# Softplus in one ScalarE instruction, and attention visits moved to odd half steps

## The chip, the cores and the metric

The kernel runs on one core of one Trainium2 chip. TensorE (PE; its weight loads are listed as PEld), VectorE (DVE), ScalarE (ACT), GpSimd (POOL) and SyncE (SP, which here only issues DMAs) each run their own instruction stream in order; semaphores tie the streams together. The metric is the device time of one execution in microseconds (us), as the median of several runs. The profile shows one execution; its times are counted from the first instruction.

## The reference

Sliding-window attention feeds a two-layer network without any normalisation in between:

```
q, k, v: 8 batches x 8 heads x 576 positions x 64
scores = q @ k.T / 8;  heads 0-3: window of 32; heads 4-7: window of 128, every 4th key
attn   = softmax(masked scores);  x = attn @ v, rearranged to 4608 tokens x 512

h  = x @ w_in                                   # 4608 x 2048
sp = max(h, 0) + log1p(exp(-|h|))               # softplus(h)
g  = h * erf(sp)
out = g @ w_out                                 # 4608 x 512
```

## The kernel before

**The network.** Tokens are cut into 9 chunks of 512. The 2048 hidden features are cut into 8 pairs of 128-wide tiles (`PAIR = 2`). One step `t` computes one such pair of tiles for one chunk; there are 72 steps (`STEPS`): the first half of chunk 0's pairs, all of chunk 1, the second half of chunk 0, and then chunks 2 to 8, eight steps each. A step consists of two half steps `j = 0, 1`. The main loop counts half steps as `x = 2t + j`, so even `x` is the first half of a step and odd `x` the second. Weights and activations are split into a high and a low part in fp32r, and each product is made of three matmuls (high x high, high x low, low x high).

In half step `x` the program issues, in this order on each engine:

- the first matmul of step `t`: `mm1` (L517) for chunks 0 to 2, or `mm1_fast` (L638) from chunk 3 on, which combines seven block products (a Strassen-like scheme) and needs 24 matmuls in the even half step and 18 in the odd one. The first half step of `mm1_fast` is x = 48;
- `take` (L659) or `take_fast` (L647 to L652), by which VectorE brings `h` out of PSUM into the tile `hc`. `h` is one PSUM tile, so that the next half step's first matmul waits for it;
- in even half steps `exponents` (L246, ScalarE): the softmax exponentials of the attention units that were scored before;
- in odd half steps `table(t - 1)` (L667, ScalarE): the erf of the step before;
- `turn` (L264, L268): transposes of the probabilities of the units that are ready, and their copy;
- `normalize` (L257, L258 on VectorE, L259 on GpSimd) of units whose exponentials are done; a unit that will be transposed in the next half step (`due`) is normalised at the end of this one;
- `gate` (L674, L677, L678, VectorE): `h * erf(...)`, split into `ghi` and `glo`;
- in odd half steps `argument(t)` (L663, L664, ScalarE);
- `weights` (`prep_act`: a cast, L440, and an Abs, L445, on ScalarE; `prep_dve`: L454 to L460 on VectorE), the 32 pieces of weight preparation, one piece per half step, done by x = 31;
- the second matmul `mm2(t - 2, j)` (L692, 12 matmuls into the accumulators `acc`), and a `store` of the output at a chunk's end;
- `attend`: `values` (L283) of the units that are ready, `scores` (L225) of new units, and `rows_hi` (L325, ScalarE), which brings the attention rows out of PSUM;
- `load_left`, `right(x)` and `build(x)`: DMA loads and preparation of the operands of `mm1_fast`. `right` makes a chunk's right-hand operands at fixed places, by x modulo 16: loads at 8, VectorE differences (L604) at 10 and 11, ScalarE casts (L608) at 11 and 12, VectorE remainders (L613) at 12, 13 and 14;
- the DMA loads `load_qk`, `load_v` of later units, `mask_max` (L236, VectorE: mask and row maximum) of the units just scored, and `rows_lo` (L331, VectorE).

In the first two steps (x = 0 to 3) the order differs: `turn` and `weights` come before the first matmul, and `attend` comes before `argument`.

**The attention.** It is cut into 72 units. Visit `n` scores unit `n` and finishes unit `n - 3` (`LAG = 3`: transposes, values, rows). Visits 0 to 13 run ahead of the main loop (`first_visit`). The function `visits` places the others by hand into half steps of the main loop: single visits 14 to 23 into x = 0 to 6, 9, 11 and 14, and after that pairs of visits. A pair scores two units and finishes two. Visits 72 to 74 only finish units.

**The activation.** Before the change, softplus is made by ScalarE as -ln(sigmoid(-h)): a Sigmoid (L663) and a logarithm (L664) over a 128x1024 tile, and the erf (L667) takes the negated argument.

Of the kernel before, what the change touches and what calls it, by code (L numbers as in the profile page):

```python
# [14 lines left out]
AF = mybir.ActivationFunctionType  # L15
# [8 lines left out]
NBLK = S // BLK  # L24
# [17 lines left out]
NU = NIT * NBLK // PER  # L42
# [8 lines left out]
REBASE = 2.0 ** -112  # L51


TINY = 1.0e-12


PAIR = 2
SPC = FT // PAIR
HALF = SPC // 2
# [6 lines left out]
LAG = 3  # L66
# [17 lines left out]
BUILD = 2 * SPC * 2 - 1  # L84
READY = 8

ANCHORS = [(0, 31), (1, 33), (2, 35), (3, 37), (4, 39), (8, 55), (13, 71), (17, 87), (22, 103)]


def paced(k):  # L90
    for (a, x), (b, y) in zip(ANCHORS, ANCHORS[1:]):
        if k <= b:
            return x + (y - x) * (k - a) // (b - a)


def visits():


    at = {n - FIRST: [n] for n in range(FIRST, 2 * NBLK + LAG)}
    n, x = 2 * NBLK + LAG, 2 * HALF + 1  # L100
    for k in range(3):
        at[x + 5 * k // 2] = [n + k]
    for k in range(3):
        at[x + 9 + 5 * k] = [n + 3 + 2 * k, n + 4 + 2 * k]
    for k, n in enumerate(range(3 * NBLK + LAG, NU + LAG, 2)):
        x = paced(k)

        at[x - (x % (2 * SPC) == 0)] = [i for i in (n, n + 1) if i < NU + LAG]
    return at


# [37 lines left out]
def attn_moe_kernel(ctx: ExitStack, tc: tile.TileContext, qk, v, masks, eye, w_in, w_out, out):  # L149
    nc = tc.nc  # L150
# [320 lines left out]
    at = {0: [[x[:, i, 0:TOK] for x in xs] for i in range(2)]}  # L471
# [182 lines left out]
    hs, ls, gs = {}, {}, {}  # L654
# [5 lines left out]

    def argument(t):

        nc.scalar.activation(out=ls[t], in_=hs[t], func=AF.Sigmoid, scale=-1.0)  # L663
        nc.scalar.activation(out=ls[t], in_=ls[t], func=AF.Ln, bias=TINY)  # L664

    def table(t):
        nc.scalar.activation(out=ls[t], in_=ls[t], func=AF.Erf, scale=-1.0)  # L667

    def gate(t, j):

# [63 lines left out]
    with tc.manual_schedule():  # L734
# [11 lines left out]
        rows_lo(FIRST - 1 - LAG)  # L746

        plan = visits()


# [9 lines left out]
        for x in range(2 * (NT + 2)):  # L760
            t, j = divmod(x, 2)
            ns = plan.get(x, [])
# [29 lines left out]
            if j == 1 and 1 <= t <= NT:  # L792
                table(t - 1)
# [12 lines left out]
            if j == 1 and t < NT:  # L806
                argument(t)
# [113 lines left out]
```

## Time and profile before

| what | value |
|---|---|
| median of 3 runs | 916.88 us (915.61 to 917.37) |
| the profiled execution: its own time | 915.3 us |
| the profiled execution: span from first to last instruction | 913.5 us |
| granted TensorE clock, mean | 0.998 |
| busy: PE / PEld / DVE / ACT / POOL | 879.1 / 756.6 / 676.9 / 663.8 / 74.3 us |

A line of a group reads: line, engine, operation, output <- input, shape, count, then busy time in all and mean ns of one, then idle time of the engine just before them and what ended it. A line of a timeline reads: start, duration, engine, line, operation, count, and in brackets the idle time before it and what ended it. A line of a table of stretches reads: the stretch in us, its length, busy time (and number of instructions) of PE, PEld, DVE, ACT and POOL, the granted TensorE clock, the DMA share and GB/s. The profile's matmuls are pipelined and their ends are modelled; so lengths of half steps are taken below from start to start of their first matmuls.

### The profile page before, as it was taken

The page shows a single profiled execution, that of the slowest core. Times are in us where ns is not written, and L with a number is a line of the kernel's source. Part 1 is how long each engine was busy: PE and PEld are TensorE (multiplying, and loading weights), DVE is VectorE, ACT ScalarE, POOL GpSimd, SP SyncE. Part 2 cuts the span into 40 slices and gives each one's busy share as a digit, 9 for nine tenths or more (in the row PEclk, how much of TensorE's full clock was granted, in tenths as well). Part 3 has the DMA queues.
Part 4 walks back from the last instruction along what each step waited for, and adds up shares of the span by engine and source line. Part 5 has one row for each costly group of instructions (what it writes and reads, how often), then busy time and mean ns, then how long its engine had stood idle before and what let it go on. Part 6 is the DMA issues. An engine that isn't in the chain of part 4 may idle for free.

```text
span 913.5 us, 22874 instructions
## 1 busy us (share of the span) xinstructions
PE 879.1 (96%) x9072; PEld 756.6 (83%) x9072; DVE 676.9 (74%) x1773; ACT 663.8 (73%) x1324; POOL 74.3 (8%) x92
## 2 busy tenths in 40 slices
PE   4788999999999999999999999999999999999998
PEld 3566877888887878888889988888988999998996
DVE  6879989986788888767776777677666866776555
ACT  7779888885878797767976687769655756655553
POOL 2311100000011100000000000000100000000000
PEclk9999999999999999999999999999999999999999
DMA  8885544531759688676657765786566546655521
GB/s 298 282 275 184 182 163 138 158 121 53 250 187 330 217 301 305 249 270 236 215 197 280 263 208 202 278 289 225 171 233 226 189 140 237 231 178 206 198 82 46
DMA packets 74059, 194.00 MB, mean 212 GB/s; under 512 B 10464, under 2 KB 22496, under 8 KB 67808
## 3 DMA queue, kind: packets, MB, share of 16 engines
q1 hardware_dynamic: 73664, 192.02, 61.6%
q8 instruction: 71, 1.16, 0.5%
q10 hardware_dynamic: 288, 0.52, 0.1%
q14 instruction: 36, 0.29, 0.1%
HBM read 155.94 MB, written 35.65 MB: 210 GB/s over the span
## 4 chain that ended last, share of the span: by engine, by line
PE 79%; DVE 9%; ACT 7%; issue 2%; DMA 1%; POOL 1%; SPq 0%; DVEq 0%; ACTq 0%; POOLq 0%
PE acc L692 36%; PE h L638 14%; PE h L517 11%; PE tx L638 10%; PE sp L283 3%; PE sp L225 3%; ACT prob L246 1%; PE sp L264 1%; DVE prob L236 1%; DMA dbl<-in_w_in_dram 1%; DVE s L674 1%; ACT L667 1%; ACT s L664 1%; DVE w L459 1%; ACT s L663 1%
## 5 line engine op out<-in xcount | busy, mean ns | idle before, releaser
L692 PE MATMUL acc<-wout_hi,ghi 128*128 128x512 f32 x576 | 228.6, 397 | 0.4 <-DVE ghi L677 0.2
L692 PE MATMUL acc<-wout_lo,ghi 128*128 128x512 f32 x576 | 225.7, 392 | 0.0
L663 ACT ACTIVATE s<-hc 128x1024 f32<-128x1024 f32 x72 | 76.3, 1060 | 171.3 <-DVE hc L652 147.7
L692 PE MATMUL acc<-wout_hi,glo 128*128 128x512 f32 x576 | 159.0, 389 | 0.0
L692 PEld LDWEIGHTS acc<-wout_hi,glo 128*128 128x128 f32 x576 | 108.1, 188 | 22.8
L692 PEld LDWEIGHTS acc<-wout_hi,ghi 128*128 128x128 f32 x576 | 108.6, 189 | 20.7 <-DVE ghi L677 1.0
L692 PEld LDWEIGHTS acc<-wout_lo,ghi 128*128 128x128 f32 x576 | 108.6, 189 | 19.6
L259 POOL TENSOR_TENSOR prob<-prob,rinv 128x256 f32<-128x256 f32 x72 | 67.8, 950 | 536.2 <-DVE ssum L257 300.8
L678 DVE TENSOR_TENSOR glo<-s,ghi 128x512 fp32r<-128x512 f32 x144 | 100.0, 694 | 5.1
L674 DVE TENSOR_TENSOR s<-hc,s 128x1024 f32<-128x1024 f32 x72 | 92.3, 1282 | 14.1 <-ACT s L667 13.9
L517 PE MATMUL h<-x,win 128*128 128x512 f32 x384 | 99.5, 402 | 2.7 <-DVE hc L659 2.6
L246 ACT ACTIVATE prob<-prob,nmax 128x64 f32<-128x64 f32 x288 | 96.3, 337 | 2.9 <-DVE nmax L236 2.6
L638 PE MATMUL h<-win 128*128 128x256 f32 x720 | 98.1, 283 | 0.0
L667 ACT ACT_TABLE_LOAD x72 | 92.4, 1283 | 1.3
L664 ACT ACT_TABLE_LOAD x72 | 92.4, 1283 | 1.3
L638 PEld LDWEIGHTS h<-win 128*128 128x128 f32 x720 | 91.6, 192 | 0.0
L517 PEld LDWEIGHTS h<-x,win 128*128 128x128 f32 x384 | 73.2, 193 | 19.4 <-DVE hc L659 3.5
L667 ACT ACTIVATE s<-s 128x1024 f32<-128x1024 f32 x72 | 76.4, 1061 | 0.8
L664 ACT ACTIVATE s<-s 128x1024 f32<-128x1024 f32 x72 | 76.3, 1059 | 0.8
L236 DVE CUSTOM_DVE_ANT_0 prob<-sp,cst 128x64 f32<-128x64 f32 x288 | 45.6, 219 | 36.1 <-ACT rows L325 26.0
L677 DVE CAST ghi<-s 128x512 fp32r<-128x512 f32 x144 | 68.1, 473 | 2.5
L651 DVE TENSOR_TENSOR hc<-tx,hc 128x512 f32<-128x512 f32 x48 | 33.0, 688 | 40.4 <-PE tx L638 40.0
(102 smaller groups left out, 1270.3 us busy)
## 6 DMA issues: line engine op xcount, KB each, us to landing
win<-ws SPq DMA_DIRECT2D x48, 1024.0 KB, 5.6
win<-ws SPq DMA_DIRECT2D x48, 768.0 KB, 4.4
v<-in_v_dram SPq DMA_DIRECT2D x72, 256.0 KB, 4.3
qk<-in_qk_dram SPq DMA_DIRECT2D x48, 272.0 KB, 4.0
dbl<-in_w_in_dram SPq DMA_DIRECT2D x16, 512.0 KB, 4.6
dbl<-in_w_out_dram SPq DMA_DIRECT2D x16, 512.0 KB, 3.6
ws<-x SPq DMA_DIRECT2D x32, 256.0 KB, 4.7
qk<-in_qk_dram SPq DMA_DIRECT2D x24, 288.0 KB, 4.5
```

The lines of the kernel that those rows point to most:

```text
L236: nc.vector.tensor_tensor_reduce(out=pr[:, g, :], in0=sps[h][:, u % 2, p, :], in1=mask[QUADS.index(kinds(u, p))], scale=-SCALE, scalar=BIG ...
L246: nc.scalar.activation(out=probs[u][:, j, :], in_=probs[u][:, j, :], func=AF.Exp, scale=-1.0, bias=nmax[:, j:j + 1], accum_out=sums[u][:, ...
L259: nc.gpsimd.tensor_tensor(probs[u], probs[u], rinv.broadcast_to([P, 2 * PARTS, KEYS]), op=ALU.mult)
L517: nc.tensor.matmul(h, win_at[:, ftp, j, cc // 2, w, cc % 2, :], x[cc], start=(k == 0 and i == 0), stop=(k == CC - 1 and i == 2))
L638: nc.tensor.matmul((h, bank)[b][:, half * HN:(half + 1) * HN], w[:, k, wi, c, :], x[:, xi, c, :], start=(c == 0 and n == 0), stop=(c == 1 ...
L663: nc.scalar.activation(out=ls[t], in_=hs[t], func=AF.Sigmoid, scale=-1.0)
L664: nc.scalar.activation(out=ls[t], in_=ls[t], func=AF.Ln, bias=TINY)
L667: nc.scalar.activation(out=ls[t], in_=ls[t], func=AF.Erf, scale=-1.0)
L674: nc.vector.tensor_tensor(out=e, in0=hc, in1=e, op=ALU.mult)
L677: nc.vector.tensor_copy(out=ghi, in_=e[:, j])
L678: nc.vector.tensor_tensor(out=glo, in0=e[:, j], in1=ghi.bitcast(F32), op=ALU.subtract)
L692: nc.tensor.matmul(acc[tt], g[:, tt * P:(tt + 1) * P], w[:, ft, :], start=(first and w is wout_hi and g is ghi), stop=(last and g is glo))
```

## The change

`argument` becomes one ScalarE instruction with the function Softplus, on `hc` itself, and `table` takes its result without the sign. The plan of visits is written out as a list `PACE` of odd half steps. The pairs that stood in even half steps or were shifted by the rule at chunk ends move: the pair of visits 24, 25 from x = 18 to 19; 28, 29 from 28 to 27; 48, 49 from 58 to 59; 52, 53 from 63 to 65; 66, 67 from 90 to 91; 70, 71 from 95 to 97. All other visits keep their half step.

```diff
-TINY = 1.0e-12
...
-ANCHORS = [(0, 31), (1, 33), (2, 35), (3, 37), (4, 39), (8, 55), (13, 71), (17, 87), (22, 103)]
...
+PACE = [19, 23, 27, 31, 33, 35, 37, 39, 43, 47, 51, 55, 59, 61, 65, 67, 71, 75, 79, 83, 87, 91, 93, 97, 99, 103]
...
-    for k in range(3):
-        at[x + 9 + 5 * k] = [n + 3 + 2 * k, n + 4 + 2 * k]
-    for k, n in enumerate(range(3 * NBLK + LAG, NU + LAG, 2)):
-        x = paced(k)
-
-        at[x - (x % (2 * SPC) == 0)] = [i for i in (n, n + 1) if i < NU + LAG]
+    for x, n in zip(PACE, range(n + 3, NU + LAG, 2)):
+        at[x] = [i for i in (n, n + 1) if i < NU + LAG]
...
     def argument(t):
 
-        nc.scalar.activation(out=ls[t], in_=hs[t], func=AF.Sigmoid, scale=-1.0)
-        nc.scalar.activation(out=ls[t], in_=ls[t], func=AF.Ln, bias=TINY)
+        nc.scalar.activation(out=ls[t], in_=hs[t], func=AF.Softplus)
 
     def table(t):
-        nc.scalar.activation(out=ls[t], in_=ls[t], func=AF.Erf, scale=-1.0)
+        nc.scalar.activation(out=ls[t], in_=ls[t], func=AF.Erf)
```

More of the change, by code (lines that the diff above doesn't have):

```diff
@@ L85 @@
 READY = 8
-ANCHORS = [(0, 31), (1, 33), (2, 35), (3, 37), (4, 39), (8, 55), (13, 71), (17, 87), (22, 103)]
[L90 to L93, printed above, removed]
+PACE = [19, 23, 27, 31, 33, 35, 37, 39, 43, 47, 51, 55, 59, 61, 65, 67, 71, 75, 79, 83, 87, 91, 93, 97, 99, 103]
 def visits():
@@ L102, in visits @@
         at[x + 5 * k // 2] = [n + k]
-    for k in range(3):
-        at[x + 9 + 5 * k] = [n + 3 + 2 * k, n + 4 + 2 * k]
-    for k, n in enumerate(range(3 * NBLK + LAG, NU + LAG, 2)):
-        x = paced(k)
-        at[x - (x % (2 * SPC) == 0)] = [i for i in (n, n + 1) if i < NU + LAG]
+    for x, n in zip(PACE, range(n + 3, NU + LAG, 2)):
+        at[x] = [i for i in (n, n + 1) if i < NU + LAG]
+    assert max(n for ns in at.values() for n in ns) == NU + LAG - 1
     return at
```

## The prediction

> **What bounds the kernel now.** I read the page's busy times and slices first, then the groups of instructions by line, then tables of stretches, and last the timeline wherever PE had idle time before a matmul.
>
> ```profile
> PE 879.1 (96%) x9072; PEld 756.6 (83%) x9072; DVE 676.9 (74%) x1773; ACT 663.8 (73%) x1324; POOL 74.3 (8%) x92
> ...
> PE   4788999999999999999999999999999999999998
> L663 ACT ACTIVATE s<-hc 128x1024 f32<-128x1024 f32 x72 | 76.3, 1060 | 171.3 <-DVE hc L652 147.7 <-DVE hc L659 23.3
> L664 ACT ACTIVATE s<-s 128x1024 f32<-128x1024 f32 x72 | 76.3, 1059 | 0.8
> L664 ACT ACT_TABLE_LOAD x72 | 92.4, 1283 | 1.3
> L246 ACT ACT_TABLE_LOAD x32 | 41.1, 1283 | 5.5 <-DVE nmax L236 3.6 <-PEq L902 0.7
> L445 ACT ACTIVATE w<-dbl 128x512 f32<-128x512 f32 x32 | 21.5, 671 | 5.5 <-DMA dbl<-in_w_in_dram 5.5
> ```
>
> PE is busy for 96% of the span, and the slices show that nearly all the rest lies in the first four (0.0 to 91 us). ScalarE, on which the change works, sits idle for 171.3 us in front of the Sigmoid alone. So 76.3 us less on ScalarE is worth nothing by itself; it is worth what it removes of the few waits of PE. In the steady part there are none:
>
> ```profile
> 693.46 0.88 PE L638 MATMUL tx<-dbl,win 128*128 128x256 f32 x6
> 698.36 1.59 PE L638 MATMUL tx<-x,win 128*128 128x256 f32 x12
> 409.65 1.59 PE L638 MATMUL tx<-win 128*128 128x256 f32 x12
> 417.65 0.97 PE L638 MATMUL tx<-win 128*128 128x256 f32 x6
> 422.65 1.59 PE L638 MATMUL tx<-win 128*128 128x256 f32 x12
> 428.27 0.88 PE L638 MATMUL tx<-win 128*128 128x256 f32 x6
> 435.56 1.69 PE L638 MATMUL tx<-win 128*128 128x256 f32 x12
> ```
>
> These are starts of half steps x = 105 and 106, and 58 to 62. Without a visit an odd half step takes 698.36 - 693.46 = 4.90 us and an even one (x = 60) 428.27 - 422.65 = 5.62. A pair of visits in an even one (x = 58) makes 8.00 there and 5.00 in the next: 2.38 + 0.10 more. A pair in an odd one (x = 61) makes 7.29: 2.39 more. Moving a pair to the other parity is therefore worth nothing in itself; what counts is only what a pair collides with.
>
> **The change, part by part.**
>
> *Softplus.* 72 Lns of 1.06 us go, the table load in front of each (1.28) now stands in front of Softplus, and the first Sigmoid's own load goes: 76.3 + 1.3 = 77.6 us off ScalarE's 663.8. The trace has no Softplus. I price it like the three functions on the same tile (1.06); the bounds are 0.67, an ACTIVATE of half the columns (L445), and 2.12, which is Sigmoid and Ln together. In the chain from `hc` to erf, 1.06 goes where ScalarE is the limit, and 2.34 where it waits for `hc`, because a load need not wait: at 57.56 below a load starts before the VectorE copy that its Sigmoid needs has ended (57.23 + 0.68).
>
> A load that is wanted before Exp is already there: 32 at L246, though each follows a Ln. The Trainium skill's page "ScalarE: Activation LUTs", section "Table sets: the hidden batching unit", says that one set holds exp and ln, so that ln and then exp need one load. By that rule Ln's departure would cost a load per group of exponentials, 31 x 1.28 = 40 us of ScalarE; this trace shows no such sharing, so I put it at nothing.
>
> *Where ScalarE is the limit: x = 1 to 4.* In order of time:
>
> ```profile
> 57.23 0.68 DVE L659 COPY hc<-h 128x512 f32<-128x512 f32 x1
> 57.56 1.28 ACT L663 ACT_TABLE_LOAD   x1
> ...
> 62.15 0.45 PE L225 MATMUL sp<-qk 64*32 64x64 f32 x32
> ...
> 66.02 0.53 ACT L325 CAST rows<-acc 128x128 fp32r<-128x128 f32 x2
> 66.30 0.68 DVE L331 TENSOR_TENSOR rows<-acc,rows 128x128 fp32r<-128x128 f32 x2 [2.81 <-ACT rows L325]
> ...
> 70.34 0.50 PE L517 MATMUL h<-x,win 128*128 128x512 f32 x1 [1.94 <-DVE hc L659]
> ```
>
> ScalarE works without a break from 57.56 to the rows at 66.02, which PE had ready at 62.6 (62.15 + 0.45). VectorE waits 2.81 for them; everything that it does up to the copy (L659) for which PE waits 1.94 is late by that. A load and an activation go (1.28 + 1.06 = 2.34), so the rows come at 63.68, still after 62.6, and the matmul at 70.34 starts 2.34 earlier, at 68.0. What is late next: VectorE still ends after PE (scores until about 67.6), so some 0.4 of wait stays. Then the clock:
>
> ```profile
> core 0: us, PE busy (x) PEld busy (x) DVE busy (x) ACT busy (x) POOL busy (x), PEclk, DMA share, GB/s
> 68.00:70.00 2.00, 0.41 (x36) 0.25 (x32) 1.93 (x4) 1.99 (x4) 0.00 (x0) 1.00 0.49 194
> 72.00:74.00 2.00, 2.00 (x6) 1.55 (x5) 1.97 (x12) 1.97 (x3) 0.16 (x1) 0.50 0.86 327
> 70.34:78.86 8.52, 8.52 (x91) 6.56 (x91) 7.91 (x25) 8.46 (x23) 1.41 (x1) 0.80 0.77 248
> 78.86:85.77 6.91, 6.91 (x100) 5.45 (x90) 5.84 (x23) 6.14 (x10) 2.03 (x2) 1.00 0.60 176
> ```
>
> Behind the gap the granted clock was 0.50 between 72 and 74 us. Half step x = 4 (70.34 to 78.86) took 8.52, and x = 5, with the same work, 6.91 at full clock: 1.61 lost. With a gap of 0.4 in place of 1.94 I expect the full clock. Together 2.34 + 1.61 = 3.95; bounds 1.06 (only Ln's time moves, the clock still falls) and 3.95.
>
> The Trainium skill's page "TensorE: Matmul & The Clock Gate", section "Why this matters for your kernels", warns of idle gaps above about 3 us; this one was 1.94 and the clock fell all the same. By the page the cause would lie elsewhere and 1.61 would stay; that is the third rival.
>
> Other stalls of this stretch I leave: those that wait for VectorE's queue or for the 5.5 us of DMA in front of L445 do not pass through Ln.
>
> *Pairs 58 and 63, 90 and 95.* Here a stall comes from a pair two half steps behind another, amid `right`'s work:
>
> ```profile
> 441.34 0.98 PE L638 MATMUL tx<-win 128*128 128x256 f32 x6
> 443.46 0.68 DVE L613 TENSOR_TENSOR win<-w,win 128x512 fp32r<-128x512 f32 x1
> 444.07 0.16 DVE L257 TENSOR_SCALAR ssum<-ssum 128x4 f32<-128x4 f32 x1
> ...
> 445.28 0.44 PE L264 MATMUL sp<-ident,prob 128*128 128x128 f32 x2 [1.30 <-POOL prob L259]
> 450.28 1.70 PE L638 MATMUL tx<-x,win 128*128 128x256 f32 x12
> 637.99 0.44 PE L264 MATMUL sp<-ident,prob 128*128 128x128 f32 x2 [1.30 <-POOL prob L259]
> 409.65:473.81 64.16, 62.86 (x859) 55.79 (x857) 48.79 (x134) 49.28 (x102) 6.19 (x7) 1.00 0.63 209
> 602.18:659.23 57.05, 55.66 (x698) 49.41 (x696) 43.45 (x125) 45.12 (x97) 6.19 (x7) 1.00 0.66 217
> ```
>
> At x = 63 the normalisation of the unit scored at 61 comes at 444.07, behind the remainders (L613), and PE's transposes wait 1.30 for it; the same at 95 (637.99). Half steps 58 to 67 took 64.16. After the change they hold the same four pairs, at 59, 61, 65, 67: 5 x 5.62 + 5 x 4.90 + 4 x 2.38 + 3 x 0.10 = 62.42, so 1.74 less. Half steps 90 to 98 (the second stretch of the table) took 57.05; with pairs at 91, 93 and 97 they take 5 x 5.62 + 4 x 4.90 + 3 x 2.38 + 3 x 0.10 = 55.14, so 1.91 less. This supposes that the new close pairs do not stall. For 59 to 61 I count from the start of 59, as an estimate. PE's scores end at 7.2, as at 61. Softplus has ended by then (`hc` comes at about 3), so rows, three casts of 0.61, a load of 1.28 and four exponentials of 0.53 with their reads follow at once and end at 13.3. VectorE, with two remainders of 0.69 in place of three, and the maximum not delayed by Ln, reaches the normalisation at 13.7; GpSimd (0.95) ends by 14.8, and PE wants the result 2.3 after its matmul at 12.9, at 15.2. So 0.4 to spare. Pairs 65, 67 and 97, 99 have no `right` work beside them.
>
> What moves with a visit: per unit a load of qk and of v and a normalisation on GpSimd (8% busy). On SP's queue they pass two loads of `load_left`. Pair 61 gets its qk loads at the end of 59, 13 us ahead; pair 63 had the same 13 to 14 after 61, without a wait. The chunks' loads at x = 56, 72, 88 and 104 rest on visits at 55, 71, 87 and 103, which do not move. Pairs 18 to 19 and 28 to 27 collide with nothing: nothing.
>
> *The end.*
>
> ```profile
> 902.27 1.22 DVE L674 TENSOR_TENSOR s<-hc,s 128x1024 f32<-128x1024 f32 x1 [2.43 <-ACT s L667]
> 904.08 0.50 PE L692 MATMUL acc<-wout_hi,ghi 128*128 128x512 f32 x1 [0.21 <-DVE ghi L677]
> ```
>
> PE's last wait, 0.21, hangs on the erf; ScalarE is over 2 us earlier there, so 0.2 goes.
>
> **Sum.** 3.95 + 1.74 + 1.91 + 0.2 = 7.8 us. Against the profiled execution's own 915.3 that gives 907.5 (span 913.5 to 905.7). The median of the runs shown, 916.88, lies 1.6 above that execution, so I predict 909.1 as the median.
>
> **Rivals.**
>
> 1. *The early stretch gains nothing*: the load or casts behind Softplus (Abs and cast, L445 and L440) need a table load each that Ln's table spared them. Two at 62 to 67 us are 2.57 against 2.34 saved. For: the trace cannot show Softplus's table. Against: in 32 cases Abs never had a load of its own, behind Exp, Ln or Erf. 909.1 + 3.95 = 913.1.
> 2. *Pairs 59, 61 and 91, 93 stall as 63 did* (8.94 - 7.29 = 1.65 each; x = 63 ran from 441.34 to 450.28): 912.4. For: three casts and two remainders stand between them, and 0.4 is little. Against: VectorE arrives there 2 us earlier than at 63. With rival 1 together: 916.4, no change.
> 3. *The clock still falls at x = 4*: 910.7. For: PE is busy for only 0.41 of the 2 us from 68 on, and visits of that kind stay. Against: x = 5, after no gap, had the full clock.
> 4. *Slower*: close pairs overload ScalarE, the erf comes late and PE waits for `ghi`. For: VectorE's 2.43 us wait for the erf at the end of the kernel shows how far `gate` can hang on it. If both pairs in `right`'s stretch cost 4.1 (1.65 and a 2.43 us later erf) and the other two 1.65: 909.1 + 11.5 = 920.6. It decides from (1.8 + 7.8) / 4 = 2.4 us per close pair on. Against: no pair loses more than 1.65 now, and ScalarE has less to do in all four places.
>
> **How the numbers follow.** Chances: forecast 0.47; rival 3 0.13, rival 2 0.14, rival 1 0.13; both 0.08; slower 0.05. Faster is 0.47 + 0.13 + 0.14 + 0.13 = 0.87, same 0.08, slower 0.05, with 0.2% (1.8 us) as about what a measurement of this kernel can tell from no change. The range reaches up to rival 1 (913.1) and 0.5 for the spread of the runs: 913.6. Downwards, stalls that I left may shrink and runs spread by 0.9: 906.4. That holds the first four cases.
>
> **What would show it.** Right: ScalarE busy near 586 us; 72 loads and 72 ACTIVATEs at `argument`; no wait above 0.5 before the first matmul of x = 4 and a clock of 1.00 there; no 1.30 waits at L264 after 430 us; half steps 58 to 67 near 62.4. Wrong: more than 176 table loads; a wait at L264 in x = 61 or 93; a Softplus longer than 1.1 us.

## The result, and the profile after

The changed kernel takes **908.94 us** in the median (908.35 to 910.76, four runs) against 917.12 (915.61 to 917.57) before: ratio **0.9917**, 95% interval 0.9899 to 0.9935. A second group of runs gave 911.17 against 917.62, 0.9924 (0.9909 to 0.994). The profiled execution took 909.18 us, with a span of 907.4.

After the change, lines stand 12 or 13 lower: L651 is the Softplus, L654 the erf, L433 the Abs and L428 the cast of the weight preparation, L505 and L626 the first matmuls, L679 the second, L252 the transposes, L224 the mask and maximum, L319 `rows_lo`, L647 the copy of `hc`. The page, busy times, slices and the groups of ScalarE:

```profile
PE 877.1 (97%) x9072; PEld 755.7 (83%) x9072; DVE 677.3 (75%) x1773; ACT 593.8 (65%) x1254; POOL 73.3 (8%) x92
...
L651 ACT ACTIVATE s<-hc 128x1024 f32<-128x1024 f32 x72 | 76.5, 1062 | 195.6 <-DVE hc L640 171.3 <-DVE hc L647 23.9
L651 ACT ACT_TABLE_LOAD x72 | 92.4, 1283 | 1.3
L654 ACT ACT_TABLE_LOAD x72 | 92.4, 1283 | 1.3
L234 ACT ACT_TABLE_LOAD x24 | 30.8, 1283 | 4.3 <-DVE nmax L224 2.6 <-PEq L889 0.7
L433 ACT ACT_TABLE_LOAD x11 | 14.1, 1283 | 0.6 <-DMA dbl<-in_w_in_dram 0.4
```

Softplus costs 1.062 us, as Sigmoid and Ln did each. ScalarE lost 70.0 us of busy time and its idle time in front of this instruction grew from 171.3 to 195.6; the span lost 6.1. There are 11 loads in front of Abs, where there were none, and 8 fewer in front of Exp.

The table of stretches of the changed kernel: x = 1 to 4, x = 3, x = 4, 58 to 67, 90 to 98, and the last one, x = 143, with all that follows it.

```profile
core 0: us, PE busy (x) PEld busy (x) DVE busy (x) ACT busy (x) POOL busy (x), PEclk, DMA share, GB/s
54.15:76.59 22.44, 20.09 (x324) 14.78 (x322) 20.97 (x75) 20.51 (x57) 2.49 (x3) 1.00 0.95 334
64.19:68.94 4.75, 4.08 (x79) 3.04 (x78) 4.25 (x13) 4.18 (x9) 0.00 (x0) 1.00 1.03 405
68.94:76.59 7.65, 7.38 (x90) 5.29 (x90) 7.48 (x24) 7.59 (x26) 1.41 (x1) 1.00 0.89 293
...
407.44:469.87 62.43, 62.43 (x859) 55.88 (x857) 48.24 (x134) 42.28 (x95) 6.19 (x7) 1.00 0.64 216
598.47:653.62 55.15, 55.15 (x697) 49.50 (x696) 42.81 (x123) 36.76 (x90) 4.17 (x5) 1.00 0.66 225
887.73:907.40 19.67, 15.98 (x79) 13.23 (x77) 9.51 (x14) 4.58 (x5) 0.00 (x0) 1.00 0.14 53
```

Before, the first of these stretches and the last took this:

```profile
53.47:78.86 25.39, 21.18 (x325) 16.03 (x324) 21.41 (x76) 23.99 (x60) 2.49 (x3) 0.93 0.84 295
...
893.34:913.51 20.17, 16.26 (x79) 13.15 (x77) 9.42 (x14) 6.93 (x7) 0.00 (x0) 1.00 0.13 52
```

So the time came from four places: x = 1 to 4, 2.95; 58 to 67, 1.73; 90 to 98, 1.90; the end, 0.50; 7.1 together. The pairs at 18 and 28 moved without a change of the sum of their two half steps and the one behind, and nearly all others are the same to 0.1 us. Of these 7.1, the span of this profile loses 0.67 to a later start of x = 0 and 0.2 to x = 88. Such shifts came in every profile (x = 0 began between 47.9 and 51.0 us in the kernels below, before any of the edits acts), and for that reason the experiments are read by half steps, start to start, and not by spans.

What was forecast for x = 4 and didn't come is in the timeline of the changed kernel:

```profile
68.94 3.02 PE L505 MATMUL h<-x,win 128*128 128x512 f32 x12 [0.57 <-DVE hc L647]
69.09 1.20 DVE L661 TENSOR_TENSOR s<-hc,s 128x1024 f32<-128x1024 f32 x1
70.32 0.72 DVE L664 CAST ghi<-s 128x512 fp32r<-128x512 f32 x1
71.07 0.69 DVE L665 TENSOR_TENSOR glo<-s,ghi 128x512 fp32r<-128x512 f32 x1
72.19 0.41 PE L252 MATMUL sp<-ident,prob 128*128 128x128 f32 x2 [0.24 <-DVE nmax L224]
72.25 0.79 DVE L319 TENSOR_TENSOR rows<-acc,rows 128x16 fp32r<-128x16 f32 x4
73.10 0.19 PEld L679 LDWEIGHTS acc<-wout_hi,ghi 128*128 128x128 f32 x1 [0.46 <-DVE rows L319]
```

The wait before the first matmul fell from 1.94 to 0.57, and the clock stayed at 1.00. But now PE waits twice more in the same half step, 0.24 and 0.46, both times for VectorE, which has worked through gate, `ghi` and `glo` first.

### The profile page after: what moved, and what is told of

The parts are those of the page before. It is cut to its first block, busy times and chain, and to the rows that moved or that the text cites. A ratio compares the mean times of both kernels' runs of the same rounds, so it can differ in the third digit from the quotient of the medians.

```text
span 907.4 us, 22834 instructions
## 1 busy us (share of the span) xinstructions
PE 877.1 (97%) x9072; PEld 755.7 (83%) x9072; DVE 677.3 (75%) x1773; ACT 593.8 (65%) x1254; POOL 73.3 (8%) x92
## 3 DMA queue, kind: packets, MB, share of 16 engines
q8 instruction: 71, 1.16, 0.5%
## 4 chain that ended last, share of the span: by engine, by line
PE 85%; DVE 9%; DMA 2%; ACT 2%; issue 1%; POOL 0%; DVEq 0%; SPq 0%; ACTq 0%; POOLq 0%
PE acc L679 40%; PE h L626 15%; PE tx L626 12%; PE h L505 10%; PE sp L271 3%; PE sp L213 3%; PE sp L252 1%; DVE w L447 1%; DVE prob L224 1%; DMA qk<-in_qk_dram 1%; DVE s L661 1%; DMA xT<-rows 1%; DVE w L448 1%; DVE hc L647 1%; DVE win L442 1%
## 5 line engine op out<-in xcount | busy, mean ns | idle before, releaser
L679 PE MATMUL acc<-wout_hi,ghi 128*128 128x512 f32 x576 | 228.5, 397 | 0.2 <-DVE dbl L697 0.2
L679 PE MATMUL acc<-wout_lo,ghi 128*128 128x512 f32 x576 | 225.6, 392 | 0.0
L651 ACT ACTIVATE s<-hc 128x1024 f32<-128x1024 f32 x72 | 76.5, 1062 | 195.6 <-DVE hc L640 171.3
L679 PE MATMUL acc<-wout_hi,glo 128*128 128x512 f32 x576 | 159.0, 389 | 0.0
L679 PEld LDWEIGHTS acc<-wout_hi,glo 128*128 128x128 f32 x576 | 108.1, 188 | 22.8
L679 PEld LDWEIGHTS acc<-wout_hi,ghi 128*128 128x128 f32 x576 | 108.6, 188 | 20.6 <-DVE dbl L697 0.6
L679 PEld LDWEIGHTS acc<-wout_lo,ghi 128*128 128x128 f32 x576 | 108.6, 189 | 19.6
L505 PE MATMUL h<-x,win 128*128 128x512 f32 x384 | 98.1, 398 | 1.3 <-DVE hc L647 1.2
L626 PE MATMUL h<-win 128*128 128x256 f32 x720 | 98.1, 283 | 0.0
L626 PEld LDWEIGHTS h<-win 128*128 128x128 f32 x720 | 91.6, 192 | 0.0
L505 PEld LDWEIGHTS h<-x,win 128*128 128x128 f32 x384 | 72.4, 191 | 17.7 <-DVE hc L647 2.2
L654 ACT ACTIVATE s<-s 128x1024 f32<-128x1024 f32 x72 | 76.3, 1060 | 0.8
L224 DVE CUSTOM_DVE_ANT_0 prob<-sp,cst 128x64 f32<-128x64 f32 x288 | 45.5, 219 | 32.0 <-ACT rows L313 21.0
L636 DVE TENSOR_TENSOR hc<-h,hc 128x512 f32<-128x512 f32 x48 | 33.2, 692 | 41.5 <-PE h L626 41.2
```

The lines of the kernel that those rows point to most:

```text
L224: nc.vector.tensor_tensor_reduce(out=pr[:, g, :], in0=sps[h][:, u % 2, p, :], in1=mask[QUADS.index(kinds(u, p))], scale=-SCALE, scalar=BIG ...
L505: nc.tensor.matmul(h, win_at[:, ftp, j, cc // 2, w, cc % 2, :], x[cc], start=(k == 0 and i == 0), stop=(k == CC - 1 and i == 2))
L626: nc.tensor.matmul((h, bank)[b][:, half * HN:(half + 1) * HN], w[:, k, wi, c, :], x[:, xi, c, :], start=(c == 0 and n == 0), stop=(c == 1 ...
L636: nc.vector.tensor_tensor(out=a[:, 0:2], in0=x, in1=a[:, 2:3].broadcast_to([P, 2, HN]), op=ALU.add)
L651: nc.scalar.activation(out=ls[t], in_=hs[t], func=AF.Softplus)
L654: nc.scalar.activation(out=ls[t], in_=ls[t], func=AF.Erf)
```

## Experiments

Each ratio is to the kernel before, timed beside it, with the 95% interval. The code cuts show each edit against the changed kernel, shortened. Where no other comparison is named, "the changed kernel" in the half steps is the profile above.

### 1. Softplus alone

```diff
-PACE = [19, 23, 27, ...]
+ANCHORS = [(0, 31), (1, 33), ...]   # the plan of visits of before
```

> Softplus in place of Sigmoid and Ln, with the plan of visits of before. Against the kernel before. My theory: the two halves of the change act in different places and add up. Softplus alone gives the early stretch (2.9 us over x = 2 to 4, with the clock at 1.00 at x = 4) and the end of the kernel (0.5), so about -3.4 us; the stalls at x = 63 and 95 stay nearly whole (8.6 to 8.9 us there, 1.0 to 1.3 of wait before the transposes of the scores), because the normalisation there queues behind VectorE's remainder work and not behind Ln. Rival: those stalls hang on ScalarE too; then x = 63 and 95 fall to about 7.3, half steps 58 to 67 to about 62.5, the whole change comes from Softplus, about -7 us, and the new plan of visits was not needed.

Measured: 911.24 us, 0.9942 (0.9927 to 0.9957). The table of stretches, x = 3, x = 4, 58 to 67, 63 alone, 90 to 98:

```profile
67.11:71.53 4.42, 3.98 (x78) 3.00 (x77) 3.98 (x9) 4.39 (x12) 0.00 (x0) 1.00 0.95 357
71.53:79.18 7.65, 7.39 (x91) 5.31 (x91) 7.48 (x24) 7.59 (x22) 1.41 (x1) 1.00 0.86 266
410.15:472.89 62.74, 62.67 (x860) 55.87 (x858) 48.73 (x134) 42.98 (x95) 6.19 (x7) 1.00 0.65 217
441.77:449.36 7.59, 7.52 (x164) 6.37 (x162) 6.44 (x14) 4.69 (x4) 2.03 (x2) 1.00 0.69 240
601.28:656.72 55.44, 55.37 (x697) 49.48 (x696) 43.38 (x125) 40.74 (x92) 6.19 (x7) 1.00 0.68 224
```

The theory fell on the stalls: x = 63 takes 7.59 in place of 8.94, and 95 the same; of the 1.65 over a pair without a stall, Softplus alone takes 1.35. The queue of VectorE shows why. First the kernel before, then Softplus alone; x = 62 begins at 435.56 and at 436.06:

```profile
434.58 1.23 DVE L674 TENSOR_TENSOR s<-hc,s 128x1024 f32<-128x1024 f32 x1 [2.25 <-ACT s L667]
```

```profile
433.86 1.23 DVE L673 TENSOR_TENSOR s<-hc,s 128x1024 f32<-128x1024 f32 x1 [1.02 <-ACT s L666]
...
443.16 0.16 DVE L257 TENSOR_SCALAR ssum<-ssum 128x4 f32<-128x4 f32 x1
...
444.38 0.20 PEld L264 LDWEIGHTS sp<-ident,prob 128*128 128x128 f32 x2 [0.31 <-POOL prob L259]
```

The normalisation comes 7.10 us after the start of x = 62, before it was 8.51. It does stand behind the remainders, but these stand behind the gate, and the gate waits for an erf that Ln had made late: it now starts 2.20 before x = 62, and 0.98 before it in the kernel before. I had followed the queue back by one step only.

The rival came nearly true. In the half steps of this profile Softplus alone gives 3.25 (x = 1 to 4, 22.14 against 25.39), 1.42, 1.61 and 0.5 (the end, 19.64 against 20.17), 6.8 of the whole change's 7.1. The times show less of it, 0.58% or 5 us; where the rest went isn't known.

### 2. The new plan of visits alone

```diff
-    nc.scalar.activation(out=ls[t], in_=hs[t], func=AF.Softplus)
+    nc.scalar.activation(out=ls[t], in_=hs[t], func=AF.Sigmoid, scale=-1.0)
+    nc.scalar.activation(out=ls[t], in_=ls[t], func=AF.Ln, bias=TINY)
```

> The new plan of visits, with Sigmoid and Ln as before. Against the kernel before. My theory: half steps 58 to 67 take 62.4 us and 90 to 98 take 55.2, 3.6 us less together; the early stretch is as before, with about 1.9 us of wait before the first matmul of x = 4 and a clock of 0.5 for some us behind it; about -3.6 us in all. Rival: the close pairs (59 and 61, 91 and 93) fit only because Softplus made ScalarE's part shorter; with Sigmoid and Ln the normalisation of 61 and 93 comes later and PE waits there up to 1.65 us each, so that the plan alone gives about 0.

Measured: 913.63 us, 0.9963 (0.995 to 0.9977). Stretches x = 3, x = 4, 58 to 67, 90 to 98:

```profile
65.21:72.02 6.81, 4.08 (x79) 3.01 (x78) 3.98 (x9) 6.77 (x20) 0.00 (x0) 1.00 0.73 289
72.02:80.53 8.51, 8.51 (x91) 6.59 (x91) 7.97 (x25) 8.45 (x23) 1.41 (x1) 0.80 0.77 248
411.78:474.22 62.44, 62.44 (x860) 55.89 (x858) 48.37 (x134) 49.31 (x102) 6.19 (x7) 1.00 0.66 220
602.88:658.03 55.15, 55.15 (x697) 49.50 (x696) 42.91 (x123) 43.20 (x96) 4.16 (x5) 1.00 0.67 223
```

As the theory said: the close pairs fit with Sigmoid and Ln too, and the early stretch is that of before. So the same two stalls have two cures. The plan alone takes 1.72 and 1.90 us from the two stretches, Softplus alone 1.42 and 1.61, both together no more than the plan (1.73 and 1.90). By the ratios the parts give 0.58% and 0.37%, both together 0.83% or 0.76%; the intervals can't tell that from a sum, the half steps can.

### 3. Sigmoid and Ln in the first step only

```diff
-    nc.scalar.activation(out=ls[t], in_=hs[t], func=AF.Softplus)
+    if t == 0:   # Sigmoid, then Ln, and a negated erf
+        ...
+    else:
+        nc.scalar.activation(out=ls[t], in_=hs[t], func=AF.Softplus)
```

> The changed kernel, but the first of the 72 steps (t = 0) has Sigmoid and Ln again. Against the changed kernel. My theory: the whole gain of the early stretch hangs on this one step, since only there ScalarE works without a break ahead of the rows of scores that VectorE and PE wait for: +2.9 us, half step x = 3 back near 6.8 us, a wait near 1.9 before the first matmul of x = 4, the granted clock at 0.5 for some us behind it, x = 4 near 8.5. Rival: the gain is spread over the first steps; then this kernel loses 1 us or less, and the clock stays at 1.00. In between: 2.1 us of the wait come back without the fall of the clock, which would say that the wait and the clock are not tied.

Measured: 912.4 us, 0.9955 (0.9943 to 0.9968). Stretches x = 1 to 4, x = 3, x = 4:

```profile
56.40:82.77 26.37, 22.10 (x325) 16.75 (x324) 21.33 (x76) 23.11 (x59) 2.49 (x3) 0.87 0.79 276
66.46:73.27 6.81, 4.05 (x78) 3.00 (x78) 3.98 (x9) 6.77 (x19) 0.00 (x0) 0.91 0.62 242
73.27:82.77 9.50, 9.50 (x91) 7.32 (x91) 7.88 (x25) 7.58 (x22) 1.41 (x1) 0.71 0.69 223
```

One of 72 instructions holds the whole early gain: x = 1 to 4 take 26.37, 3.93 more than with 72 Softplus. That is one microsecond more than expected, and more than before the change (25.39): here the low clock lasted two of its windows (below), and x = 4 took 9.50 in place of 8.51.

### 4. Softplus twice

```diff
-    nc.scalar.activation(out=ls[t], in_=hs[t], func=AF.Softplus)
+    for _ in range(2 if t >= 4 else 1):
+        nc.scalar.activation(out=ls[t], in_=hs[t], func=AF.Softplus)
```

> The changed kernel with Softplus executed twice in steps 4 to 71, 68 x 1.06 = 72 us more on ScalarE, on the same operands, so that the output is the same. Against the changed kernel. My theory: ScalarE is off the path in the steady part (195.6 us of idle time in front of Softplus), so ScalarE's busy time goes from 594 to about 666 us and the time moves by less than 2 us: what is left comes at the close pairs (59 and 61, 91 and 93), with at most 1.3 each, and at the end, 0.5. Rival: ScalarE's time counts by its length; then the kernel gets slower by something like a tenth of 72 us or more.

Measured: 910.68 us, 0.9934 (0.9912 to 0.9955). Busy times, then the stretches 5 to 57, 58 to 67, 68 to 142 and the end:

```profile
PE 877.9 (96%) x9072; PEld 756.4 (83%) x9072; DVE 677.8 (74%) x1773; ACT 664.9 (73%) x1322; POOL 74.4 (8%) x92
```

```profile
78.84:409.83 330.99, 326.98 (x3286) 270.58 (x3277) 270.59 (x730) 270.74 (x550) 33.64 (x34) 1.00 0.61 207
409.83:472.27 62.44, 62.44 (x860) 55.89 (x858) 48.37 (x134) 48.60 (x101) 6.20 (x7) 1.00 0.65 219
472.27:890.18 417.91, 417.88 (x3642) 376.71 (x3637) 288.87 (x627) 281.41 (x440) 16.63 (x18) 1.00 0.63 214
890.18:909.83 19.65, 15.96 (x79) 13.23 (x77) 9.42 (x14) 5.64 (x6) 0.00 (x0) 1.00 0.14 53
```

ScalarE has 71.1 us more to do. The changed kernel takes 76.59 to 407.44 = 330.85, 62.43, 469.87 to 887.73 = 417.86 and 19.67 in the same stretches; 0.18 us is all that comes back, and nothing of it at the end, where I had expected 0.5. What this profile has more lies ahead of the doubled instructions (x = 2, where the values waited 2.87 for a load of v, and the clock fell after it).

### 5. Copy in place of Abs

```diff
-    nc.scalar.activation(out=w, in_=d[:, :, 1].bitcast(F32), func=AF.Abs, scale=REBASE)
+    nc.scalar.activation(out=w, in_=d[:, :, 1].bitcast(F32), func=AF.Copy, scale=REBASE)
```

> The changed kernel with a scaled Copy in place of the scaled Abs in front of the bit operations at `weights` (the sign is shifted out by them anyway). Against the changed kernel. My theory: Abs is what needs a table of its own behind Softplus, Copy needs none; the 11 loads at that line go, and up to 8 come back at Exp, so 168 to 176 table loads in place of 179; the time does not move (within 1 us), because the 3 loads more than before lie in ScalarE's idle time. In x = 2 to 4, where ScalarE works without a break, at most one load (1.28) goes, which could bring up to 0.5 us. Rival (that of the prediction): these loads are what the early stretch lost against the forecast; then x = 2 to 4 get 1.0 us shorter.

Measured: 910.07 us, 0.9926 (0.991 to 0.9943). Groups, then x = 1 to 4:

```profile
L234 ACT ACT_TABLE_LOAD x32 | 41.1, 1283 | 9.5 <-DVE nmax L224 7.6 <-PEq L889 0.7
L433 ACT ACTIVATE w<-dbl 128x512 f32<-128x512 f32 x32 | 21.5, 670 | 6.5 <-DMA dbl<-in_w_in_dram 6.5
```

```profile
54.83:77.00 22.17, 20.01 (x324) 14.75 (x322) 20.92 (x75) 20.78 (x57) 2.49 (x3) 1.00 0.93 317
```

All 11 loads at the Abs go and 8 come back at Exp: 176, the number predicted. No time comes of it: 22.17 for x = 1 to 4 lies beside 22.44 and 22.16 of the changed kernel's two profiles. The timelines of x = 2 show why: in the changed kernel the load in front of Abs (61.14) serves the exponentials behind it as well, and with Copy the same load stands in front of these (62.38).

### 6 to 8. The waits that are left

Three single edits to the changed kernel. The first puts the loop that normalises units due in the next half step ahead of `load_left`, `right` and `build`:

```diff
+            for u in [u for u in scaled if due[u] == x + 1]:
+                scaled.remove(u)
+                normalize(u)
             load_left(t + 2, j)
             right(x)
             build(x)
```

> The changed kernel with the early normalisation (of a unit whose values are due in the next half step) put ahead of the loads, the right side's work and the building of W in VectorE's queue. Against the changed kernel. My theory: the waits of the transposes at x = 35, 37 and 39 (0.17, 0.64 and 0.18 in the changed kernel, half steps of 8.28, 8.72 and 8.26 against 7.88 without a wait) come from VectorE's queue order, as those of 63 and 95 did; they go, and the three half steps take 7.9, so -1.0 to -1.6 us. Rival: the maximum is itself not there yet when the normalisation is wanted, or what is pushed back (building W, the right side) stalls PE elsewhere: 0 or slower by up to 2 us.

The second moves two pairs of visits:

```diff
-PACE = [..., 37, 39, 43, 47, 51, ...]
+PACE = [..., 37, 39, 41, 49, 51, ...]
```

> The changed kernel with the pairs of visits of x = 43 and 47 at 41 and 49. Against the changed kernel. My theory: the pair at 47 is what costs the last 1.65 of that kind: half step 46 takes 6.45 against 5.59 without a wait, and 47 takes 8.88 against 7.88 of a pair. With the pair at 49, half steps 40 to 50 give 1.8 us back. Rival: 46 and 47 wait for the right side's first chunk (VectorE's differences at x = 42 to 46), whatever the visits; then 46 keeps its 6.45 and nothing changes, or 49, in the first fast half steps, stalls in its place; or the pair at 41, two half steps behind 39, stalls as 37 and 39 do (0.4 to 0.9 more).

The third moves the maximum and the low rows forward in the first two steps:

```diff
+            if t < 2:   # moved here from behind build(x)
+                for n in scored:
+                    mask_max(n)
+                    todo.append(n)
+                for m in ready:
+                    rows_lo(m)
             if j == 1 and 1 <= t <= NT:
                 gate(t - 1, 0)
```

> The changed kernel with the maximum of the scores and the low rows of x = 3 put ahead of the gate of step 0 in VectorE's queue. Against the changed kernel. My theory: what the early stretch gave less than forecast (2.93 of 3.95) is VectorE: its gate (1.20), ghi (0.72) and glo (0.69) stand ahead of the low rows for which the first matmul of the output (0.46) and the transposes (0.24) of x = 4 wait. In this order both waits go or shrink and x = 4 takes 7.0 to 7.2 us in place of 7.66, so -0.4 to -0.7 us in the half steps. Rival: VectorE's work is only shuffled, and the same matmul waits for ghi instead; x = 4 stays at 7.5 or more.

Measured: 909.31 us, 0.9917 (0.99 to 0.9935); 907.98, 0.9908 (0.9891 to 0.9925); 909.84, 0.9924 (0.9903 to 0.9946). By the times none of them can be told from the changed kernel. By half steps all three do what was said, the second only in part. With the normalisation first, x = 37:

```profile
278.16:286.04 7.88, 7.88 (x157) 6.43 (x155) 7.40 (x17) 6.25 (x14) 2.31 (x2) 1.00 1.02 358
```

35, 37 and 39 take 7.88 or 7.89 each, 1.6 less together. With the pairs moved, 46 takes 5.57 in place of 6.45 and 47 and 49 together 12.72 in place of 13.78, but 41 stalls behind 39 (8.28, as 35 and 39 did): both theory and the third branch of the rival, so that half steps 40 to 50 give 1.4 back (66.96 to 65.58) and not 1.8. With the scores first, x = 4:

```profile
71.06:78.18 7.12, 7.12 (x91) 5.48 (x91) 6.95 (x24) 7.08 (x21) 0.61 (x1) 1.00 0.92 292
```

7.12 in place of 7.65; the second matmul there now waits 0.18, for `ghi`. So 0.5 of the part of the early gain that was missing was VectorE's order.

### 9 to 12. All orders together, with 72, no and one Softplus

First the edits of experiments 5 to 8 in one kernel:

> The changed kernel with all four edits together: Copy for Abs, the early normalisation first, pairs at 41 and 49, the scores' maximum ahead of the gate at x = 3. Against the changed kernel on the same chip. My theory: the three gains in PE's half steps lie in different places and add up: 1.63 (x = 35, 37, 39), 1.77 (x = 46 to 49, with 41 at 7.88 now, since the normalisation comes first) and 0.54 (x = 4), 3.9 us together; half steps 10 to 57 take 295.1 in place of 298.5. Rival: as with the two parts of the change, they overlap, and together they give no more than the larger two thirds of it, 2.6 us or less.

Beside it the changed kernel, unedited:

> The changed kernel itself, beside the others on the same chip. Theory and rival: 0.9917 of the kernel before, within 0.1%, as in its first comparison; against it the other two of this group are read.

Then the four edits with Sigmoid and Ln:

```diff
-    nc.scalar.activation(out=ls[t], in_=hs[t], func=AF.Softplus)
+    nc.scalar.activation(out=ls[t], in_=hs[t], func=AF.Sigmoid, scale=-1.0)
+    nc.scalar.activation(out=ls[t], in_=ls[t], func=AF.Ln, bias=TINY)
```

> All four edits of order and visits, but Sigmoid and Ln in place of Softplus. Against the kernel with all four edits and Softplus. My theory: with the queues in this order Softplus is still worth what only ScalarE can give: the stretch x = 3 and 4 with the fall of the clock (3 to 4 us) and the end (0.5), so this kernel is 3.5 to 4.5 us slower, and half steps 5 to 142 take the same time within 0.5 us. Rival 1: with VectorE's order mended, ScalarE's part is hidden everywhere, and the difference is under 1 us. Rival 2: Softplus is also what lets the normalisation come early enough elsewhere; then waits of the transposes come back at 35 to 39, 59 to 67 or 91 to 97 and the difference is over 5 us.

And last with `if t == 0:` Softplus, else Sigmoid and Ln:

> All four edits of order and visits, with Softplus in step 0 alone and Sigmoid and Ln in the other 71 steps. Against the kernel with all four edits and 72 Softplus, by their ratios to the kernel before. My theory: of the 72 instructions one matters besides the last; ScalarE is busy some 76 us longer, half steps 1 to 4 are as with 72 Softplus (x = 3 near 4.5, no fall of the clock unless a load of v comes late), the end is 0.5 longer, and the ratio is the same within 0.1% (0.989 to 0.991). Rival: the 1.3 us that the kernel with 72 Ln and these orders lost is spread over the steps; then half steps 5 to 142 take 0.5 us or more longer, and the early stretch brings nothing.

Measured: all four edits 907.85 us, 0.9895 (0.9878 to 0.9912), beside 911.17, 0.9924 (0.9909 to 0.994) of the changed kernel on the same chip, 3.3 us less; with Sigmoid and Ln in all steps 909.14, 0.991 (0.9892 to 0.9927); with Softplus in step 0 only 907.28, 0.9899 (0.9879 to 0.992). Half steps 10 to 57, first of the changed kernel in that group, then with the edits:

```profile
111.31:409.71 298.40, 295.04 (x2969) 245.29 (x2959) 241.18 (x647) 216.89 (x466) 27.16 (x27) 1.00 0.62 210
```

```profile
113.72:408.53 294.81, 293.80 (x2969) 245.25 (x2959) 242.54 (x647) 213.72 (x463) 28.95 (x27) 1.00 0.63 213
```

3.59 less there, near the 3.4 expected (1.63 and 1.77; the rest is 0.2 at x = 14). x = 4 itself takes 7.23 in place of 7.65, but x = 1 to 4 together don't show it (24.50 against 22.16): the load of v came 3.02 us late at x = 2 in this profile, and the clock fell behind it. These edits lie at different places and add up, unlike the two parts of the change. By its ratio it is the fastest version here, though its interval just overlaps the changed kernel's.

With Sigmoid and Ln the same orders lose 1.3 us, less than the 3.5 expected, nearer to the first rival, and within the intervals. So the orders and the plan of visits without Softplus can't be told from the changed kernel. In its profile x = 3 is 2.2 longer than in the changed kernel's second profile (6.68 against 4.46) and the end 0.5, as expected, but the clock did not fall at x = 4. With one Softplus in place of 72 the ratio moves by 0.0004, while ScalarE is busy for 662.0 us. That fits the theory, but it doesn't show it, since the ratio with none (0.991) lies within the same intervals. The profile of this kernel doesn't show it either. Its x = 1 to 4, and 5 to 142:

```profile
53.54:77.47 23.93, 21.21 (x325) 16.08 (x323) 20.42 (x75) 20.36 (x54) 1.69 (x3) 0.93 0.89 301
77.47:886.12 808.65, 806.51 (x7780) 703.08 (x7771) 610.19 (x1489) 597.14 (x1093) 59.10 (x58) 1.00 0.63 212
```

x = 1 to 4 take 23.93 against 24.02 with no Softplus, because the load of v came 2.50 us late here and the clock fell behind it. And 5 to 142 take 808.65 against 807.48 with 72 Softplus, more than the 0.5 that the rival named; 0.84 of it lies at x = 14, which took from 7.69 to 8.59 us in the profiles here, and 8.59 with 72 Softplus in experiment 7. What the first step's instruction is worth is shown by experiment 3; that it is worth as much as all 72 stays open.

## Why the prediction was right, point by point

It said 909.1 us, and 908.94 came. The agreement is partly luck: its 7.8 us are 7.1 in the half steps, while the medians lie 8.2 apart in this group and 6.5 in the second.

**The early stretch** is the term that was mis-sized: 3.95 forecast, 2.95 measured (3.23 in the second profile, 22.16 against 25.39). The mechanism held: Ln and its load stood ahead of the rows, the wait before the first matmul of x = 4 fell to 0.57 (0.4 said, and "no wait above 0.5" as a sign), the clock stayed up. One size was off. The start came 2.08 earlier in the first profile and 2.36 in the second, for the 2.34 forecast. But x = 4 took 7.65 in both, where I had taken x = 5's 6.91 for it: "with the same work" holds for PE but not for VectorE, which there has a gate and the low rows in its queue. Experiment 8 gave 0.53 of these 0.74 by order alone. That the clock would stay up was right for a reason that holds only in part (rival 3). And one line was misread, without harm: the rows come from the values, which ended at 62.2, and not from the scores, which ended at 62.6.

**The pairs** came out to a hundredth: 62.43 for 62.42 and 55.15 for 55.14, with no wait at the transposes. But the reason given was half of the truth. Experiment 1 shows that Ln was a cause of these stalls as well as the place of the visits, so 3.03 of these 3.63 came from Softplus without any move. And the spare time of the close pairs, which I had tied to Softplus, is there without it (experiment 2).

**The end** gave 0.50, where I had 0.2. The last stretch shortened by more than its last wait.

**Rival 1** was right in its premise and wrong in its price: Abs does need a load of its own behind Softplus, 11 times, so there are 179 loads and not 176 ("more than 176" was named as a sign against me), and ScalarE's 593.8 us are 7.8 above the 586 said, of which 4.3 go in experiment 5; the rest isn't accounted for. In x = 2 the load at Abs stands in place of the one at Exp, so that a load and an activation went all the same, as forecast. Experiment 5 takes the loads at Abs away without a gain. The argument "in 32 cases Abs never had a load" was drawn from tables that were not Softplus's. The 40 us of further loads in front of Exp, which the prediction put at nothing, did not come: Exp's loads went down, from 32 to 24.

**Rivals 2 and 4** didn't come: no close pair stalled, and even 71.1 us more of ScalarE hurt none.

**Rival 3** did not come in the two profiles of the changed kernel, but what decided it was not what I had said. Where the granted clock fell, it fell for whole windows of 3.41 us, at another offset in each profile. The windows below are counted in steps of 3.41 us from the changes of the clock in the same profile (the fourth from its fall at the end of the kernel): before; Softplus absent, visits moved; Ln in step 0 only (two windows in sequence); all orders with Ln.

```profile
68.16:71.57 3.41, 1.48 (x37) 1.13 (x19) 3.31 (x7) 3.38 (x8) 0.82 (x1) 1.00 0.52 154
```

```profile
69.91:73.32 3.41, 1.47 (x31) 1.09 (x8) 3.31 (x6) 3.38 (x8) 0.90 (x1) 1.00 0.53 138
```

```profile
68.63:72.04 3.41, 1.88 (x68) 1.22 (x66) 2.75 (x7) 3.38 (x9) 0.00 (x0) 1.00 0.62 243
72.04:75.45 3.41, 2.18 (x5) 1.79 (x6) 3.31 (x7) 3.38 (x7) 1.41 (x1) 0.50 0.52 135
```

```profile
70.01:73.42 3.41, 1.67 (x7) 1.41 (x8) 3.34 (x18) 3.38 (x8) 0.62 (x1) 1.00 0.93 283
```

All four have the same gap of 1.94 us before x = 4. After the first two windows the clock went to 0.50 for one window (3.41 us), after the third for two, after the last not at all. So the gap's length alone doesn't decide. How long PE is busy in a window goes with the clock, but isn't the whole rule. The clock also fell behind windows with 0.54, 0.92 and 1.16 us of PE (experiment 4, Softplus in step 0 only, all four edits), and it stayed up behind windows with 2.08 (experiment 1), 2.18 and 2.81 (the changed kernel, the windows that end at 68.85 and 68.87). But it fell behind 1.88 and stayed up behind 1.67. What else counts is not shown; the window with 1.88 holds 64 small matmuls of the attention, the one with 1.67 holds only matmuls on 128 rows.

Where the windows lie differs from profile to profile, so the clock's part of the gain comes in some executions and not in others. In the group timed beside experiments 9 and 10, four runs of the kernel before had a mean clock of 0.996 and took 918.45 to 919.65 us; the five with 0.998 to 1.000 took 916.01 to 917.62.

The Trainium skill's page "TensorE: Matmul & The Clock Gate", in "Part 1: The HAM clock gate", gives such a window, free-running, with 3413 ns; the low stretches here, 3.41 and 6.83 us, agree with it. By its table an idle window lowers the clock; here windows did that in which PE was busy for 0.54 to 1.88 us.

**Left open.** In four of the later profiles the load of v at x = 2 came late (waits of 1.75 to 3.02 us against 0.86); edits that act only later had it too, and why it varies wasn't tried. What a window must hold to keep the clock isn't set by these rows.

## What to carry to other kernels

Time taken off an engine that is not the bound is worth what it removes from the few places where the bound waits: look for those places and price each, since here one of 72 identical instructions held the whole early gain, 2.95 of 7.1 us. When a stall is charged to one engine's queue, follow that queue back for more than one instruction before you say what would cure it; two cures of one stall don't add up. And compare half steps, start to start, when a change is under one per cent: most of them repeat so well that they showed effects of 0.5 us where medians of the same kernel lay 2 apart; a few, here x = 0, 2, 3, 14 and 88, don't.

## What the hardware showed unasked

- A table load for Abs (1.283 us, 11 times) appeared behind Softplus and none for a scaled Copy in the same place (32 Copies of 670 ns, no load).
- The granted clock changed in steps of 3.41 us, and behind the same gap of 1.94 us it fell in three profiles and not in a fourth.
- A table load didn't wait for the data of its activation, so that it hid where ScalarE waits. In the changed kernel:

```profile
883.74 1.28 ACT L651 ACT_TABLE_LOAD   x1
890.81 1.06 ACT L651 ACTIVATE s<-hc 128x1024 f32<-128x1024 f32 x1 [5.79 <-DVE hc L640]
```
